# A bound for the first head from key maxima and weight-column lengths, with the opening of an attention kernel re-ordered around it

## The chip, the cores and the metric

The kernel runs on one core of a Trainium2 chip. A core has TensorE (PE, with its weight loads listed as PEld), VectorE (DVE), ScalarE (ACT), GpSimd (POOL) and SyncE (SP), which run side by side and wait for each other through semaphores, and 16 DMA engines. The metric is the device time of one execution in microseconds; the lower the better. Times of the timeline below are microseconds from the first instruction of the profiled execution.

## The reference

```python
xn = layernorm(x)                                   # x: 2048 x 640, eps 1e-5, no gain or offset
q = (xn @ wq).reshape(B, Sq, 32, 192).transpose(0, 2, 1, 3)
scores = einsum("bhqd,bhkd->bhqk", q, k_cache) * 192 ** -0.5
p = softmax(scores)
o = einsum("bhqk,bhkd->bhqd", p, v_cache)           # 32 heads, 2048 cached keys and values of 192
s = o.transpose(0, 2, 1, 3).reshape(B, Sq, 32 * 192) @ wo
h = silu(x @ w1) * (x @ w3)                         # called with xn in the place of x; 1536 wide
g = silu(h @ w2)
out = x + s * g
```

All tensors are bfloat16. x and the caches are normal numbers times 0.05; `wq` is normal times 0.05 over the root of 640.

## The kernel before, in words

**Softmax with a bound.** The kernel doesn't look for the maximum of each row of scores. It computes one number per head that no score exceeds in size, subtracts it inside the exponential, and divides by the sum of the exponentials at the end (the ones column of `vt` collects that sum). The bound is the sum over the 192 dimensions of (largest |k| of the dimension) x (largest |q| of the dimension), times the scale 192 ** -0.5 and a slack of 1.03. A second, exact path at the end of the program (`redo`) runs only where a sum of exponentials has become too small.

**Tiling.** Keys of a head are held transposed in `KT`, 128 partitions x 3 x 1024. Since 192 isn't a multiple of 128, two keys share a column: block 0 holds dimensions 0 to 127 of the even keys, block 1 dimensions 128 to 191 of the even keys and 0 to 63 of the odd ones, block 2 dimensions 64 to 191 of the odd ones. `KM` holds the two half blocks that have to lie on the other 64 partitions; POOL copies them (`copy_low` L139, `copy_high` L142). Queries are made per chunk of 512 rows of x: `project_chunk` (L348) multiplies the weights with `xnT`, the normalised and transposed x, and leaves `qA` (dimensions 0 to 127), `qF` (dimensions 128 to 191, beside 64 columns of the feed-forward weights), and copies on other partitions `qS` and `qD`. A step of attention is a pair of key tiles: `scores` (L508) is three pairs of 64-row matmuls into a PSUM tile `st2` of 1024 columns, `weights` (L530) is one exponential of it on ACT, and `values` (L561) are 32 matmuls of 193 columns that use the exponentials as weights. One block is eight such steps (512 queries against 2048 keys); a head has four blocks, and there are 32 heads. `advance` (L587) keeps the values two or three halves behind the scores.

**PSUM.** `st2` tiles come from a ring of two and serve the scores, the projections (`ps`) and the transposes of x (`pst`). The tags `ob0` and `ob1` hold the value sums; before the first values they serve other things: `ob1` is `fill`, the target of matmuls that only keep PE going, then `ahead`, then `third`; `ob0` is `bp`, half of the first projection.

**What sets the order.** Nearly every instruction of the first head is pinned (`pin`), so each engine issues in the order in which the program lists it. Each engine has one queue, SP and POOL issue DMAs from theirs, and an instruction that waits holds everything behind it.

**The opening.** x is loaded by tiles of 128 rows. DVE takes mean and variance (`ln_stats`), ACT makes the reciprocal root by a Ln and an Exp (`ln_root`), DVE scales (`ln_scale`), and PE and ACT transpose (`ln_turn`). Tiles 0 to 3 make chunk 0. `lead` (L648) runs the first five steps of head 0 and between them prepares tiles 4 to 7; tiles 8 to 15 are transposed by DMA from SP (`ln_send` L289) for later chunks. Chunk 0 of head 0 is projected at L363, 20 matmuls of 256 columns; then five matmuls `ahead` (L619) make `qA` of head 1's chunk 0. The first bound takes the key maxima (L404, DVE), the query maxima of chunk 0 straight from PSUM (L393), a shift between partition halves on POOL (`turned_shift` L425), their product (`first_product`), and a matmul with ones that sums over partitions and leaves the sum on all of them (`first_bound` L459). Chunks 1 to 3 get bounds of their own from `next_bound` (L479), with an all-reduce over partitions on POOL (L476). `posts` and `extra_at` (L679, L689) list what is put behind which step: chunk 1 is projected at step (0, 5), head 1's first chunk at (1, 1).

Of the kernel before, what the change touches and what calls it, by code (L numbers as in the profile page):

```python
# [30 lines left out]
def _kernel_impl(ctx, tc, A_x, A_k_cache, A_v_cache, A_wq, A_wo, B_w1, B_w3, B_w2, out):  # L31
# [57 lines left out]
    def load_weights(h):  # L89
# [5 lines left out]
        if h == 0:  # L95
# [7 lines left out]
            return dict(wq=(columns(1), columns(0)), next_wA=columns(2),  # L103
                        pieces=[lambda: piece(A_wq[:, 0:DH + P], PGW, PGW + DH + P), lambda: piece(wsel[:, 0:PGW], 0, PGW)])
# [54 lines left out]
    with ExitStack() as actx:  # L159
# [44 lines left out]
        def load_cols(out, w):  # L204
            pin(nc.gpsimd.dma_start(out=out, in_=w.rearrange("(c p) d -> p c d", p=P)))

        loads[0] = load_keys(0, [first_w["pieces"][0], lambda: [f() for f in first_w["pieces"][1:]], lambda: [load_x(nc.sync, *t) for t in ((4, 6), (6, 8), (8, 12))]])
        loads[0].update(first_w)
        load_x(nc.sync, 12, 16)
# [107 lines left out]
        def start_head(h):  # L317
# [9 lines left out]
            pin((nc.gpsimd if h == 1 else nc.vector).memset(heads[h]["st"][:], 0.0))  # L327
# [20 lines left out]
        def project_chunk(h, qb, cast=nc.vector.tensor_copy, mid=()):  # L348
# [8 lines left out]
            elif h == 0:  # L357
                acc["bp"] = ps_o.tile([P, 2, 512], F32, tag="ob0", name="bp")
# [20 lines left out]
            else:  # L379
                pin(cast(out=qA[:, qs], in_=halves[0]))  # L380
                pin(cast(out=qF[:, qs], in_=halves[1]))
            keep = pin if h == 0 or h == 1 else (lambda x: x)
            first = h == 0 and qb == 0
            copy = nc.scalar.copy if first else nc.gpsimd.tensor_copy
            for t in range(2):
                keep((copy if t == 0 else nc.gpsimd.tensor_copy)(out=qS[ROWS[t], qs], in_=qA[ROWS[1 - t], qs]))  # L386

            keep(copy(out=qD[:, qs], in_=qF[PGW:P, qs]))

            def maxima():  # L390
                cA, cF = (4, 3) if h == 0 else (3, 4)
                for col, src, r0 in ((cA, halves[0] if first else qA[:, qs], 0), (cF, halves[1] if first else qF[:, qs], PGW)):
                    pin(nc.vector.tensor_reduce(out=st[r0:P, col, qb:qb + 1], in_=src[r0:P, :], axis=AX.X, op=ALU.max,  # L393
                                                apply_absolute_value=True))
# [30 lines left out]
        def turned_shift():  # L425
            m = heads[0]["st"][:, 0:3, 0]
            sh = stt.tile([P, 2], F32, tag="sh", name="sh")
            pin(nc.gpsimd.memset(sh[ROWS[0], 0:1], 0.0))

            def down():  # L430
                pin(nc.gpsimd.tensor_copy(out=sh[ROWS[1], 1:2], in_=m[ROWS[0], 1:2]))

            def rest():
                pin(nc.gpsimd.tensor_copy(out=sh[ROWS[0], 1:2], in_=m[ROWS[1], 0:1]))
                pin(nc.gpsimd.tensor_copy(out=sh[ROWS[1], 0:1], in_=m[ROWS[0], 0:1]))  # L435

            def join():
                km = stt.tile([P, 2], F32, tag="km", name="km")
                pin(nc.vector.tensor_tensor(out=km[:], in0=m[:, 1:3], in1=sh[:], op=ALU.max))
                return km  # L440
            return down, rest, join

# [9 lines left out]
        def first_product():  # L452
            hd = heads[0]
            pr = stt.tile([P, 2], BF16, tag="prb", name="prb")
            pin(nc.vector.scalar_tensor_tensor(out=pr[:], in0=hd["km"][:], scalar=-SCALE * SLACK,
                                               in1=hd["st"][:, 3:5, 0], op0=ALU.mult, op1=ALU.mult))
            return pr

        def first_bound(pr):  # L459
            hd = heads[0]  # L460
            bp = acc["bp"]
            for t in range(2):
                pin(nc.tensor.matmul(bp[:, 0, 0:1], lhsT=ones_bf[:], rhs=pr[:, t:t + 1], start=(t == 0), stop=(t == 1)))
            nb = stt.tile([P, 1], F32, tag="nbb", name="nbb")
            pin(nc.vector.tensor_copy(out=nb[:], in_=bp[:, 0, 0:1]))
            hd["nb"] = [nb]
# [11 lines left out]

        def next_bound(qb):  # L479
# [717 lines left out]
```

## Time and profile before

| | us |
|---|---|
| median of 3 runs | 1936.65 |
| lowest and highest of them | 1936.47, 1936.83 |
| the profiled execution | 1935.99 |
| span of the profiled execution, first to last instruction | 1934.4 |
| PE busy | 1927.3 |
| ACT busy | 1214.5 |
| DVE busy | 1090.5 |
| POOL busy | 460.1 |

The granted clock of TensorE was 1.00 throughout. A row of the timeline gives start, duration, engine, source line, operation, output and inputs with partitions x elements, how many were merged into it (x), and in brackets the idle time of the engine just before it and what ended that. Matmuls are pipelined: a matmul's shown duration includes the time in which its results drain while the next one already streams, so the distance of starts tells what one costs. A few matmul records are missing from the trace. The chain that ended last is found by going back from the last instruction, at each step to what released it or to the instruction before it on its engine. Groups by line give count, busy time in all, mean duration in ns, and the idle time before them.

### The profile page before, as it was taken

Reading aid. Unit: us, or ns where it says so; the run is one execution under the profiler, and the core shown is the slowest. Engines: PE = TensorE matmul, PEld = TensorE weight load, DVE = VectorE, ACT = ScalarE, POOL = GpSimd, SP = SyncE. Lnnn points to the kernel's source line nnn. Section 1 sums busy time; section 2 is a strip of 40 time slices with the busy share of each in tenths; the row PEclk is TensorE's granted clock in tenths of the full one; section 3 lists DMA queues with packets and bytes.
Section 4 is the critical chain, followed back from the end, with each engine's and each line's share of the span. In section 5 each row is a group of like instructions: output and inputs, shape, how many; then the busy total and the mean of one; then the engine's idle time right before and its main releaser. Section 6 shows DMA issues by size and latency. Waiting matters only on the chain.

```text
span 1934.4 us, 59509 instructions
## 1 busy us (share of the span) xinstructions
PE 1927.3 (100%) x26711; PEld 1264.6 (65%) x26734; DVE 1090.5 (56%) x2239; ACT 1214.5 (63%) x1177; POOL 460.1 (24%) x759
## 2 busy tenths in 40 slices
PE   9999999999999999999999999999999999999999
PEld 5666666666666666666667766666666666454446
DVE  8665656565656565666655666656665655521111
ACT  7777777777767677777777777777777777210000
POOL 3532222222222222233222222222222220000000
PEclk9999999999999999999999999999999999999999
DMA  7721223121212222232222222212131102937763
GB/s 172 140 71 42 80 42 79 42 73 37 59 40 66 51 56 62 58 95 68 63 50 71 50 71 48 73 42 79 41 79 35 46 10 84 268 92 143 167 147 82
DMA packets 339810, 148.62 MB, mean 77 GB/s; under 512 B 290384, under 2 KB 333008, under 8 KB 339552
## 3 DMA queue, kind: packets, MB, share of 16 engines
q1 hardware_dynamic: 326496, 115.00, 25.7%
q0 software_dynamic: 8352, 24.75, 4.8%
q10 hardware_dynamic: 4704, 5.05, 0.8%
q8 instruction: 209, 3.42, 0.8%
q14 instruction: 49, 0.40, 0.1%
HBM read 54.59 MB, written 31.98 MB: 45 GB/s over the span
## 4 chain that ended last, share of the span: by engine, by line
PE 99%; SPq 0%; DMA 0%; ACT 0%; issue 0%; DVE 0%; POOL 0%
PE obank L572 35%; PE st L526 34%; PE ps L374 14%; PE ps_s L941 8%; PE ps_s L897 3%; PE ps_f L961 2%; PE ps_gu L754 1%; PE ps_f L977 1%; PE ps L779 0%; PE ps L338 0%; DMA KT<-in_A_k_cache_dram 0%; SPq L119 0%; PE ps_gu L338 0%; ACT xnT L281 0%; PE pst L280 0%
## 5 line engine op out<-in xcount | busy, mean ns | idle before, releaser
L532 ACT ACTIVATE pT<-st,nb 128x1024 bf16<-128x1024 f32 x1016 | 1130.6, 1113 | 435.4 <-PE st L526 435.0
L572 PEld LDWEIGHTS <-pT 64*128 64x128 bf16 x16384 | 713.3, 94 | 243.0 <-ACT pT L532 1.9
L572 PE MATMUL obank<-vt,pT 64*128 64x193 bf16 x16384 | 852.4, 243 | 0.2 <-ACT pT L532 0.2
L542 DVE COPY osum<-obank 128x386 f32<-128x386 f32 x256 | 142.2, 556 | 551.3 <-PE obank L572 551.3
L526 PE MATMUL st<-qS,KM 64*128 64x512 bf16 x1023 | 384.7, 376 | 0.1
L526 PE MATMUL st<-qA,KM 64*128 64x512 bf16 x1023 | 384.7, 376 | 0.0
L526 PE MATMUL st<-qA,KT 64*128 64x512 bf16 x1023 | 384.7, 376 | 0.0
L526 PE MATMUL st<-qS,KT 64*128 64x512 bf16 x1023 | 384.7, 376 | 0.0
L526 PE MATMUL st<-qF,KT 64*128 64x512 bf16 x1023 | 384.7, 376 | 0.0
L526 PE MATMUL st<-qD,KT 64*128 64x512 bf16 x1023 | 384.6, 376 | 0.0
L386 POOL COPY qS<-qA 64x512 bf16<-64x512 bf16 x255 | 188.8, 741 | 503.8 <-DVE qA L380 478.1
L526 PEld LDWEIGHTS <-KT 64*128 64x128 bf16 x4096 | 201.6, 94 | 136.1 <-issue 0.6
L374 PE MATMUL ps<-xnT,wq 64*128 64x512 bf16 x1230 | 285.7, 376 | 0.0
L374 PE MATMUL ps<-xnS,wq 64*128 64x512 bf16 x1230 | 284.6, 376 | 0.0
L374 PEld LDWEIGHTS <-wq 64*128 64x128 bf16 x2460 | 119.2, 94 | 115.6
L549 DVE TENSOR_TENSOR ostage<-osum,rl_all 128x384 bf16<-128x384 f32 x256 | 152.6, 596 | 8.8
L941 PE MATMUL ps_s<-oT,wo_sb 128*128 128x512 bf16 x705 | 154.9, 379 | 0.8
L543 DVE TENSOR_TENSOR osum<-osum,obank 128x386 f32<-128x386 f32 x256 | 142.6, 557 | 8.9
L941 PEld LDWEIGHTS <-wo_sb 128*128 128x128 bf16 x720 | 70.4, 98 | 84.9 <-issue 0.2
L404 DVE TENSOR_REDUCE st<-KT 128x1 f32<-128x512 bf16 (+1 forms) x189 | 122.1, 685 | 1.4 <-DMA KT<-in_A_k_cache_dram 0.2
L526 PEld LDWEIGHTS <-KM 64*128 64x128 bf16 x2048 | 100.6, 94 | 16.2 <-POOL sh L435 0.4
L108 POOL DMA_DIRECT2D wq<-in_A_wq_dram x62 | 45.5, 734 | 272.5 <-PE ps L374 250.6
(148 smaller groups left out, 1180.9 us busy)
## 6 DMA issues: line engine op xcount, KB each, us to landing
o_scr<-ostage SPq DMA_DIRECT2D x64, 384.0 KB, 2.7
vt<-in_A_v_cache_dram SPq DMA_DIRECT2D x62, 384.0 KB, 4.9
wo_sb<-in_A_wo_dram POOLq DMA_DIRECT2D x1, 7680.0 KB, 31.7
wq<-in_A_wq_dram POOLq DMA_DIRECT2D x31, 160.0 KB, 3.2
hT_scr<-hblk SPq DMA_DIRECT2D x16, 256.0 KB, 3.1
xnS<-xnT POOLq DMA_DIRECT2D x8, 320.0 KB, 5.7
wq<-in_B_w_dram POOLq DMA_DIRECT2D x31, 80.0 KB, 2.6
wq<-in_A_wq_dram POOLq DMA_DIRECT2D x31, 80.0 KB, 2.9
```

The costliest lines, as they stand in the source:

```text
L108: keep(nc.gpsimd.dma_start(out=wq[ROWS[t], :, c0:c1], in_=w.rearrange("(s p) d -> p s d", p=DT)))
L374: pin(nc.tensor.matmul(halves[t], lhsT=wq[ROWS[t], s, :], rhs=xs[ROWS[t], s // 2, qs], start=(s == 0), stop=(s == 2 * DC - 1)))
L386: keep((copy if t == 0 else nc.gpsimd.tensor_copy)(out=qS[ROWS[t], qs], in_=qA[ROWS[1 - t], qs]))
L404: pin(nc.vector.tensor_reduce(out=heads[h]["st"][:, j, k:k + 1], in_=heads[h]["L"]["KT"][:, j, c0:c1], axis=AX.X, op=ALU.max, apply_absolu ...
L526: pin(nc.tensor.matmul(st2[:, t * 512:(t + 1) * 512], lhsT=k, rhs=q[ROWS[t], qs], start=(s == 0), stop=(s == 2)))
L532: pin(nc.scalar.activation(out=pT2[:], in_=st2[:], func=ACT.Exp, scale=SCALE, bias=nb[:]))
L542: pin(nc.vector.tensor_copy(out=osum[:], in_=ov[:, 0, :, 0:DH + 1]))
L543: pin(nc.vector.tensor_tensor(out=osum[:], in0=osum[:], in1=ov[:, 1, :, 0:DH + 1], op=ALU.add))
L549: pin(nc.vector.tensor_tensor(out=ostage[:, b * 2:b * 2 + 2, hg * DH:(hg + 1) * DH], in0=osum[:, :, 0:DH], in1=rl.unsqueeze(2).to_broadcas ...
L572: pin(nc.tensor.matmul(acc["o"][b][:, r, (j % 2) * 256:(j % 2) * 256 + DH + 1], lhsT=pT2[ROWS[r], t * 512 + j * P:t * 512 + (j + 1) * P], ...
L897: pin(nc.tensor.matmul(ps, lhsT=oT[:, k, :], rhs=wo_sb[:, k, c0:c1], start=(k == 0), stop=(k == OC - 1)))
L941: pin(nc.tensor.matmul(ps_of[d], lhsT=wo_sb[:, k, d * P:(d + 1) * P], rhs=part(k // KQ)[:, k % KQ, :], start=(k == 0), stop=(k == OC - 1)))
```

## The change

The bound of head 0 no longer looks at queries. A row of the normalised x has a squared length of at most 640, so no |q| of a dimension exceeds the root of 640 times the length of that dimension's column of `wq`. The lengths come from squares of the weights (ACT for 128 columns, POOL for 64), 20 one-column matmuls against ones that sum the squares over the 640 rows, and a Ln and an Exp with factor one half for the root. One bound then holds for all four chunks of head 0, so the query maxima of head 0, the shift between partition halves and `next_bound` go. Even and odd keys get sums of their own, in two banks of `fill`, and the smaller of the two (the larger bound, since they are negative) is taken.

Around that:

- `ahead` goes into the second half of the projection's own tile `ps`, which is unused since the other half of the projection is in `bp`; before, it had a tile of its own in `ob1`.
- For chunk 0 the two `qS` copies run on DVE (before: one on ACT, one on POOL) and the `qD` copy on POOL (before: ACT).
- For chunk 1 of head 0 the cast of `qF` runs on DVE (before: ACT).
- The scaling and transposes of tiles 8 and 9 (`ln_send` 8) and the second half of tile 11's statistics move from inside and behind the projection of chunk 1 to behind step (0, 5).
- `next_wF` and the weights of head 1 are loaded from SP's queue (before: POOL's), `next_wF` ahead of the last x tiles and the weights behind them; x tiles 8 to 15 come in five pieces instead of two.
- The warm-up all-reduce on POOL now takes `wn`, and it and the first `swap_rows` stand before the first scores (before: after the third step).
- The memset of head 0's `st` goes.

```diff
-                keep(nc.gpsimd.dma_start(out=wq[ROWS[t], :, c0:c1], in_=w.rearrange("(s p) d -> p s d", p=DT)))
+                keep((nc.sync if h == 1 else nc.gpsimd).dma_start(out=wq[ROWS[t], :, c0:c1], in_=w.rearrange("(s p) d -> p s d", p=DT)))
...
-        loads[0] = load_keys(0, [..., lambda: [load_x(nc.sync, *t) for t in ((4, 6), (6, 8), (8, 12))]])
+        loads[0] = load_keys(0, [..., lambda: [load_x(nc.sync, *t) for t in ((4, 6), (6, 8), (8, 10), (10, 12))]])
         loads[0].update(first_w)
-        load_x(nc.sync, 12, 16)
+        load_cols(next_wF[:, :, 0:PGW], B_w3[:, 0:PGW])
+        load_cols(next_wF[:, :, PGW:P], A_wq[:, DH + P:2 * DH])
+        for t0, t1 in ((12, 14), (14, 15), (15, 16)):
+            load_x(nc.sync, t0, t1)
+        loads[1] = load_weights(1)
...
-                pin(cast(out=qF[:, qs], in_=halves[1]))
+                pin((nc.vector.tensor_copy if h == 0 and qb == 1 else cast)(out=qF[:, qs], in_=halves[1]))
...
-                keep((copy if t == 0 else nc.gpsimd.tensor_copy)(out=qS[ROWS[t], qs], in_=qA[ROWS[1 - t], qs]))
-            keep(copy(out=qD[:, qs], in_=qF[PGW:P, qs]))
+                keep((nc.vector if first else nc.gpsimd).tensor_copy(out=qS[ROWS[t], qs], in_=qA[ROWS[1 - t], qs]))
+            keep(nc.gpsimd.tensor_copy(out=qD[:, qs], in_=qF[PGW:P, qs]))
...
+        def weight_squares():
+            wq = first_w["wq_all"][:, :, PGW:PGW + DH]
+            sq = lnx.tile([P, DC, DH], BF16, name="sq")
+            pin(nc.scalar.activation(out=sq[:, :, DT:DH], in_=wq[:, :, DT:DH], func=ACT.Square))
+            pin(nc.gpsimd.tensor_tensor(out=sq[:, :, 0:DT], in0=wq[:, :, 0:DT], in1=wq[:, :, 0:DT], op=ALU.mult))
+            return sq
+
+        def weight_norms(sq):
+            ns = fill[:, 1, 0:3]
+            for rows_, j, k0 in ((slice(0, P), 2, DT), (slice(0, P), 0, 0), (ROWS[0], 1, P), (ROWS[1], 1, 0)):
+                for c in range(DC):
+                    pin(nc.tensor.matmul(ns[rows_, j:j + 1], lhsT=sq[:, c, k0:k0 + rows_.stop - rows_.start], rhs=ones_bf[:, 0:1],
+                                         start=(c == 0), stop=(c == DC - 1)))
+            lw = stt.tile([P, 3], F32, tag="lw", name="lw")
+            pin(nc.scalar.activation(out=lw[:], in_=ns, func=ACT.Ln, bias=eps_t[:], scale=1.0))
+            wn = stt.tile([P, 3], F32, tag="wn", name="wn")
+            pin(nc.scalar.activation(out=wn[:], in_=lw[:], func=ACT.Exp, scale=0.5))
+            return wn
+
+        def first_product(wn):
+            pr = stt.tile([P, 3], BF16, tag="prb", name="prb")
+            pin(nc.vector.scalar_tensor_tensor(out=pr[:], in0=heads[0]["st"][:, 0:3, 0], scalar=-SCALE * SLACK * float(D) ** 0.5,
+                                               in1=wn[:], op0=ALU.mult, op1=ALU.mult))
+            return pr
...
+            sums = [fill[:, t, 8:9] for t in range(2)]
             for t in range(2):
-                pin(nc.tensor.matmul(bp[:, 0, 0:1], lhsT=ones_bf[:], rhs=pr[:, t:t + 1], start=(t == 0), stop=(t == 1)))
+                pin(nc.tensor.matmul(sums[t], lhsT=ones_bf[:], rhs=pr[:, 2 * t:2 * t + 1], start=True, stop=False))
+            for t in range(2):
+                pin(nc.tensor.matmul(sums[t], lhsT=ones_bf[ROWS[t], :], rhs=pr[ROWS[t], 1:2], start=False, stop=True))
             nb = stt.tile([P, 1], F32, tag="nbb", name="nbb")
-            pin(nc.vector.tensor_copy(out=nb[:], in_=bp[:, 0, 0:1]))
-            hd["nb"] = [nb]
+            pin(nc.vector.tensor_reduce(out=nb[:], in_=fill[:, :, 8], axis=AX.X, op=ALU.min))
+            heads[0]["nb"] = [nb] * NQB
...
+        sq = weight_squares()
         copy_low(L0)
         key_maxima(0, 0)
-        rest_of_shift()
-        project_chunk(0, 0, nc.scalar.copy)()
-        heads[0]["km"] = join()
+        project_chunk(0, 0, nc.scalar.copy)
         set_ones(L0)
...
         start_head(1)
-        pr = first_product()
-        ahead = ps_o.tile([P, 2, 512], F32, tag="ob1", name="ahead")
+        wn = weight_norms(sq)
+        warm = stt.tile([P, 1], F32, tag="warm", name="warm")
+        pin(nc.gpsimd.partition_all_reduce(warm[:], wn[:, 0:1], P, bass_isa.ReduceOp.add))
+        swap_rows(0)
+        pr = first_product(wn)
+        ahead = acc["ps"][:, 512:1024]
...
-        early = [scores(heads[0], 0, 0)]
-        first_bound(pr)
+        early = [scores(heads[0], 0, 0, hook=lambda: first_bound(pr))]
...
         posts = {
-            (0, 5): ((ln_send, 10, 1),),
+            (0, 5): ((ln_send, 8), (ln_send, 10, 1), (ln_half, 11, 1)),
...
-            (0, 5): ((first_project, 0, 1, (ln_root, 8, 3), (ln_send, 8)),),
+            (0, 5): ((first_project, 0, 1, (ln_root, 8, 3)),),
```

The hook of the first `scores` runs `first_bound` between its first and its second pair of matmuls.

More of the change, by code (lines that the diff above doesn't have):

```diff
@@ L423, in join_maxima @@
             return km
[L425 to L441, printed above, removed]
         def key_shift(h):
@@ L506, in swiglu_chunk, with scores @@
             return product
-        def scores(hd, qb, p, fill=(0, 0, 0), st2=None):
+        def scores(hd, qb, p, st2=None, hook=None):
             KT, KM = hd["L"]["KT"], hd["L"]["KM"]
@@ L523, in scores @@
             for s, step in enumerate(steps):
-                keep_busy(fill[s])
+                if hook and s == 1:
+                    hook()
                 for t, (k, q) in enumerate(step):
@@ L636, in first_project @@
             maxima = project_chunk(h, qb, nc.scalar.copy, mid)
-            if h == 0:
-                maxima()
-                if qb == 1:
-                    ln_half(11, 1)
-                next_bound(qb)
-            else:
+            if h:
                 behind.append(maxima)
@@ L656, in lead @@
             ln_root(4, 4)
-            warm = stt.tile([P, 1], F32, tag="warm", name="warm")
-            pin(nc.gpsimd.partition_all_reduce(warm[:], rstd[4], P, bass_isa.ReduceOp.add))
-            heads[1]["L"].update(load_weights(1))
-            swap_rows(0)
             st2 = scores(hd, 0, 4)
```

33 lines of the change are left out of this document (9 added, 24 removed).

## The prediction

> **What bounds the kernel now.** I read the busy line and the chain that ended last first, then the chain in order of time, and then the rows of the first 45 us, because only there does the order of instructions change: behind head 0 every engine's list is the same as before.
>
> ```profile
> span 1934.4 us, 59509 instructions
> PE 1927.3 (100%) x26711; PEld 1264.6 (65%) x26734; DVE 1090.5 (56%) x2239; ACT 1214.5 (63%) x1177; POOL 460.1 (24%) x759
> ...
> PE 99%; SPq 0%; DMA 0%; ACT 0%; issue 0%; DVE 0%; POOL 0%
> ```
>
> TensorE (PE) is busy for 1927.3 of 1934.4 us and carries 99% of the chain. One row of the chain in order of time, repeated, shows the steady pace:
>
> ```profile
> 74.86 2.16 PE ps L374 x20
> 87.53 2.16 PE ps L374 x20
> ```
>
> A block of eight key pairs takes 87.53 - 74.86 = 12.67 us, all of it on PE. Work taken off VectorE (DVE), ScalarE (ACT) or GpSimd (POOL) gains there only where PE waits for it, and a TensorE instruction added is paid in full unless it stands in such a wait. So the sum is made of two stretches in which PE does wait: from the first projection to the first exponentials, and from 26 to 31 us. The first, by start and duration in the timeline:
>
> ```profile
> 11.91 0.58 ACT L380 CAST qA<-ps 128x512 bf16<-128x512 f32 x1 [1.01 <-PE ps L363]
> 12.26 1.24 PE L619 MATMUL ahead<-xnT,wq 128*128 128x512 bf16 x4
> 13.29 0.61 POOL L386 COPY qS<-qA 64x512 bf16<-64x512 bf16 x1
> 13.43 0.39 PE L526 MATMUL st<-qA,KM 64*128 64x512 bf16 x1
> 13.52 0.70 DVE L393 TENSOR_REDUCE st<-bp 64x1 f32<-64x512 f32 x1
> 13.96 0.37 PE L526 MATMUL st<-qS,KM 64*128 64x512 bf16 x1
> 14.11 0.57 ACT L620 CAST qA<-ahead 128x512 bf16<-128x512 f32 x1
> 14.69 0.20 PE L463 MATMUL bp<-prb,ones_bf 128*128 128x1 bf16 x2
> 14.93 0.16 DVE L465 COPY nbb<-bp 128x1 f32<-128x1 f32 x1 [0.33 <-PE bp L463]
> 15.13 2.12 ACT L532 ACTIVATE pT<-st,nbb 128x1024 bf16<-128x1024 f32 x2 [0.44 <-DVE nbb L465]
> 16.30 0.51 PE L572 MATMUL obank<-vt,pT 64*128 64x193 bf16 x8
> ```
>
> PE has finished `ahead` at about 13.3 and issues the first score pair in halves, at 13.43 and 13.96, because its second half needs `qS`, whose POOL copy ends at 13.90. The bound is late too: query maxima on DVE until 14.22, product, PE at 14.69, copy until 15.09, and only then the first exponential (15.13). PE gets its first weights at 16.30. A 512-column matmul is shown with 0.37 to 0.39 but gives way sooner: `ahead` is five matmuls (one record is missing) from 12.26 to 13.50, so four steps to the last start and one duration of 0.38 make a step (1.24 - 0.38) / 4 = 0.215 us.
>
> **The change, stretch one.** Added on PE: 20 matmuls of one column each (norms of the weight columns) between the projection and `ahead`, and four instead of two for the bound. Added on ACT: one square over 640 elements a partition, a Ln, an Exp. Added on POOL: a product over 320 elements. Their nearest rows:
>
> ```profile
> 5.30 0.29 ACT L253 ACTIVATE lv<-mv,eps_t 128x1 f32<-128x1 f32 x1 [0.31 <-DVE mv L225]
> 5.63 0.20 ACT L260 ACTIVATE rstd<-lv 128x1 f32<-128x1 f32 x1
> 5.74 0.81 ACT L243 ACTIVATE junk<-x_all,nmean 128x640 bf16<-128x640 bf16 x1
> 11.70 1.04 POOL L139 COPY KM<-KT 64x1024 bf16<-64x1024 bf16 x1 [1.14 <-DMA KT<-in_A_k_cache_dram]
> 18.30 2.18 PE L572 MATMUL obank<-vt,pT 64*128 64x193 bf16 x48
> 20.41 1.32 PE L280 MATMUL pst<-ident_bf,xn 128*128 128x128 bf16 x20
> ```
>
> The square costs about 0.81 (the square of 128x640). ACT is idle for 1.01 before its cast at 11.91, so it lies in that gap at no cost; if it ran over by 0.2, the cast would be late by that and nothing would wait, since DVE reads `qA` only after its key maxima at about 12.9. The POOL product has no row. POOL has been idle for 1.14 before the second key copy at 11.70; a copy of 1024 elements takes 1.04, so 320 elements with two inputs are bounded by about 0.3 and 1.0, both hidden; a longer one would push that key copy, which ends at 12.74, some 1.5 before PE reads it.
>
> The 20 one-column matmuls have no row as a group. Each loads its own weights. From below, the 48 of 193 columns take 2.18, or 0.045 each, two side by side. From above, the pair at 14.69 gives way to the next scores at 14.83 (the row of 14.69 says 0.20 for both with their tail), and 20 transposes take 1.32 or 0.066 each. That is 0.9 to 1.3 us; I take 0.9, as one column streams less than the 193 that make up the lower row. A smaller cost isn't excluded, so the low end of the range uses 0.5, the nearest row halved. The Trainium skill, TensorE: Matmul & The Clock Gate, section "Back-to-back issue gap", gives about 81 ns for a stream of weight load and matmul at 128 columns, and its section "Wait — 56ns, not 53.3ns?" a floor of about 25 ns between starts; as estimates these would be 1.6 and 0.5 us here. The transposes at 0.066 speak against the first of them.
>
> With N for that time the order after it is: `ahead` 12.26+N to 13.34+N (five steps of 0.215), the first score pair until 13.55+N, four bound matmuls at 0.045 until 13.73+N, two pairs until 14.16+N, readable 0.17 later. The Ln (0.29) and Exp (0.20) run beside `ahead`; the product of 0.16 follows at about 13.2+N, ahead of its use at 13.55+N; the minimum over both banks ends near 14.1+N. The first exponential therefore starts at 14.37+N, set by the scores and no longer by the bound: 15.27 with N = 0.9, against 15.13. What was a wait for `qS` and for the bound is now filled with norms. The two `qS` copies move to DVE behind its key maxima, 12.9 to about 13.6, in time for 13.34+N; `qD` moves to POOL after `qF` at 13.05, there by 13.7 to 14.1 and needed at 13.94+N. `ahead` in the free half of `ps` makes the second score tile wait until ACT has copied it (13.5+N plus 0.57): 14.1+N, when PE arrives at 14.16+N. Stretch one: **+0.14**, ends -0.3 (N = 0.5) and +0.5 (N = 1.3). The layer norm chain behind it follows ACT's exponentials and shifts by the same.
>
> **Stretch two.** The rows from 26 to 31, and the cast on DVE from the groups by line:
>
> ```profile
> 25.94 0.58 ACT L380 CAST qA<-ps 128x512 bf16<-128x512 f32 x1 [0.29 <-PE ps L338]
> 26.43 0.59 ACT L381 CAST qF<-ps 128x512 bf16<-128x512 f32 x1
> 26.66 1.25 POOL L386 COPY qS<-qA 64x512 bf16<-64x512 bf16 x2
> 26.90 2.14 ACT L532 ACTIVATE pT<-st,nbb 128x1024 bf16<-128x1024 f32 x2
> 27.07 0.37 PE L526 MATMUL st<-qA,KM 64*128 64x512 bf16 x1
> 27.97 0.61 POOL L388 COPY qD<-qF 64x512 bf16<-64x512 bf16 x1
> 28.00 0.49 DVE L223 BATCH_NORM_STATS2 st<-x_all 128x6 f32<-128x320 bf16 x1
> 28.09 0.51 PE L572 MATMUL obank<-vt,pT 64*128 64x193 bf16 x8 [0.19 <-ACT pT L532]
> 28.53 0.21 DVE L225 BATCH_NORM_AGGREGATE mv<-st 128x2 f32<-128x12 f32 x1
> 29.49 0.45 DVE L271 TENSOR_SCALAR xn<-x_all,mv,rstd 128x640 bf16<-128x640 bf16 x1 [0.19 <-ACT rstd L260]
> 29.58 2.13 ACT L532 ACTIVATE pT<-st,nb 128x1024 bf16<-128x1024 f32 x2
> 29.61 1.45 POOL L386 COPY qS<-qA 64x512 bf16<-64x512 bf16 x2
> 30.75 1.26 PE L368 MATMUL ps<-xnT,next_wF 64*128 64x512 bf16 x10
> ```
>
> ```profile
> L381 DVE CAST qF<-ps 128x512 bf16<-128x512 f32 x120 | 81.6, 680 | 0.0
> ```
>
> Half the cast of chunk 1 (0.59 on ACT) goes to DVE, where it takes 0.68. It starts after ACT's `qA` cast at 26.53 (in the changed order its one wait is for ACT) and ends at 27.23, not 27.02. ACT's exponential starts at 26.55, not 26.90, so the wait of PE at 28.09 goes: 27.66 is early enough. But three things come next. The score tile that reuses the projection's bank, issued at 27.07, must now wait for DVE: 27.28. It ends at 27.93, so PE gains only 28.09 - 27.93 = 0.16. Second, on DVE the normalisations of tiles 8 to 10 (0.45 each, 0.36 apart) no longer run before the cast but behind it, until 28.4, then the half statistics (0.49) and the aggregate (0.21), so `mv` is ready at 29.1 and not at 28.74. Third, ACT holds its exponentials behind the Ln of that `mv`: Ln at 29.15, exponential at 29.6, where it now starts at 29.58. The projection at 30.75 waits for the bank that this exponential frees. So the gain of 0.16 is lost again at 30.75: **0.0** if nothing else happens. The removed all-reduces of the query bound only took 0.1 of ACT's wait there.
>
> What else can happen is that DVE and POOL hold each other up. POOL's copies of `qS` take 1.25 for two at 26.66 but 1.45 at 29.61, where the first begins 0.12 after a normalisation has begun on DVE (29.49): 0.20 longer. In the new order three normalisations stand exactly over `qS` and `qD` (27.3 to 28.6). The Trainium skill, SBUF — State Buffer, section on who interferes with whom, says that such a VectorE instruction and any GpSimd one exclude each other for the whole instruction; 0.20 here agrees with it. Bounds from the rows: none, 0.0; one hold of 0.20 for each of two pairs moves `mv` by 0.4 and so the projection to 31.15; if the two engines alternate in full, DVE loses two copies of about 0.5 and the projection comes 1.1 late. I take the middle, **+0.4**.
>
> **Parts without a price.** Eight query reductions (0.70 each) leave DVE and three all-reduces POOL; PE waited for none of them after 30 us. The warm-up all-reduce and the two swaps go ahead of the weights' loads, from 22.6 and 25.2 to about 14; POOL is idle there and the next POOL work that PE needs is `qS` at 26.66. SP issues the 128 columns of `next_wF` and the three pieces of head 1 weights instead of POOL, and x in smaller pieces: five more issues of 0.5 ahead of the transposes of tiles 8 on, whose first was issued at 26, so they fall in SP's idle time. The value rows of pairs 4 to 7 are issued 0.5 later and now share the engines with the swaps:
>
> ```profile
> 11.54 1.06 SPq L122 DMA_DIRECT2D vt<-in_A_v_cache_dram  x2
> 21.67 0.51 PE L572 MATMUL obank<-vt,pT 64*128 64x193 bf16 x8
> ```
>
> ```profile
> DMA to landing us min/median/max: 3.9/5.0/6.2
> ```
>
> They landed at most 6.2 after issue, that is by 18.3, and are read from 21.67: 3.4 us of cover. Without that cover each further us would be one on PE. The transposes of tiles 8 to 11 start 1.5 later, but no longer beside the weight loads; used at 35.8.
>
> **Sum.** +0.14 + 0.4 = +0.5. The profiled execution took 1935.99 (span 1934.4 and 1.6 around it), 0.66 under the median of 1936.65; it would be 1936.5, and the median **1937.2 us**. About 0.2% (3.9 us) is what counts here as a difference, so this is no change.
>
> **Rivals.** (a) No net effect, 1936.65 within 0.3: the norms take 0.75 and DVE and POOL don't meet. For: PE's share of 100%; against: the row at 29.61. (b) Faster, 1935.9: N = 0.5 (-0.3), no holds, and the transfer of the cast keeps 0.4 since the exponential isn't behind the Ln; for: the wait of 0.4 before 28.09; against: the order on ACT. It can't reach 0.2%, as PE's waits in the two stretches (about 0.5 around 13.43 to 13.96, 0.2 at 14.69, 0.2 at 16.30, 0.4 at 28.09) sum to about 1.3, and 0.5 must be paid. (c) Slower: the swaps and weights put ahead hold back the value rows. It decides where these take over 9.6 us to land (12.05 to 21.67): at twice the longest, 12.4, PE stands still for 2.8 us, 1939.9, and at 13.8 it would be over 0.2%. Against: 6.2 was the most. (d) Full alternation in stretch two with N = 1.3: +1.6, 1938.2.
>
> **Chances.** Forecast (+0.2 to +1.2) 0.48; (a) 0.22; (b) 0.15; (d) 0.10; (c) 0.05, of which 0.03 beyond 0.2%. For 8 in 10 the range takes in (a), (d) and most of (b): 1935.8 to 1938.3. Faster by over 0.2% 0.015, the same 0.95, slower 0.035.
>
> **What the changed profile would show.** Right: the norms end about 0.9 after 12.26, no split first score pair, the first exponential at 15.2 to 15.4; a POOL copy near 27.3 longer than 0.8, the Ln of tile 11 after 29.1, and the projection of `next_wF` at about 31.3. Wrong: norms under 0.6 or over 1.4; POOL copies of 0.61 throughout with the projection before 30.7; PE idle before 21.67 on value rows; any difference behind 45 us, where the block should still take 12.67.

## The result and the profile after

The changed kernel takes 1948.49 us (median; 1945.11 to 1951.60), the kernel before 1936.56 beside it: a ratio of 1.0061, interval 1.0048 to 1.0074. It is slower by 12 us, where no change was forecast. The page of the changed kernel, its busy line, its chain by engine and one group by line:

```profile
span 1946.9 us, 59553 instructions
PE 1931.4 (99%) x26756; PEld 1332.2 (68%) x26756; DVE 1085.6 (56%) x2226; ACT 1214.9 (62%) x1177; POOL 452.8 (23%) x748
PE 98%; DMA 1%; DVE 0%; ACT 0%; POOL 0%; issue 0%; POOLq 0%
L380 PE MATMUL ps<-xnS,wq 64*128 64x512 bf16 x1230 | 283.1, 378 | 9.2 <-DMA xnS<-xnT 9.2
```

The span has grown by 12.5 us, the busy time of PE by 4. The share of DMA in the chain has risen from 0% to 1%, and the group says which transfer it is: the projections of later heads, which read `xnS` (the normalised x with its halves of partitions swapped), waited 9.2 us for the DMA that writes it. In the kernel before the same group has no wait:

```profile
L374 PE MATMUL ps<-xnS,wq 64*128 64x512 bf16 x1230 | 284.6, 376 | 0.0
```

The timeline of PE puts the wait in one place, head 1's projection of chunk 3 at step (3, 4); first the kernel before, then the changed one:

```profile
65.96 0.38 PE L374 MATMUL ps<-xnT,wq 64*128 64x512 bf16 x1
65.97 0.59 PE L374 MATMUL ps<-xnS,wq 64*128 64x512 bf16 x2
...
67.91 0.38 PE L374 MATMUL ps<-xnT,wq 64*128 64x512 bf16 x1
```

```profile
66.23 0.38 PE L380 MATMUL ps<-xnT,wq 64*128 64x512 bf16 x1
75.76 0.61 PE L380 MATMUL ps<-xnS,wq 64*128 64x512 bf16 x2 [9.15 <-DMA xnS<-xnT]
76.13 0.66 PE L380 MATMUL ps<-xnT,wq 64*128 64x512 bf16 x2
76.56 0.66 PE L380 MATMUL ps<-xnS,wq 64*128 64x512 bf16 x2
...
79.54 0.38 PE L380 MATMUL ps<-xnT,wq 64*128 64x512 bf16 x1
```

Until there the change has cost 0.27 us (66.23 against 65.96). The first matmul on `xnS` comes 9.79 later than before, so the wait is worth 9.5. Then the nine pairs up to the last row take 3.78 us instead of 1.94, a pair each 0.42 instead of 0.215: another 1.84. At 79.54 the kernel is 11.63 behind, and that is nearly all of the 12.5. The windows of the changed kernel (busy time of PE, PEld, DVE, ACT, POOL, then the granted clock, the DMA engines' busy share and GB/s) show both terms:

```profile
55.00:60.00 5.00, 5.00 (x86) 3.52 (x82) 1.59 (x4) 4.42 (x5) 4.84 (x7) 1.00 1.25 208
60.00:65.00 5.00, 5.00 (x74) 3.10 (x70) 4.82 (x10) 3.36 (x5) 4.08 (x8) 1.00 1.28 113
65.00:70.00 5.00, 1.60 (x25) 0.89 (x22) 1.47 (x4) 2.08 (x2) 0.08 (x1) 0.93 1.30 105
70.00:75.00 5.00, 0.00 (x0) 0.00 (x0) 0.00 (x0) 0.00 (x0) 0.00 (x0) 0.50 0.62 119
75.00:80.00 5.00, 4.24 (x24) 1.77 (x25) 0.00 (x0) 0.04 (x1) 0.00 (x0) 0.55 0.06 14
```

PE, DVE, ACT and POOL stand still from 70 to 75, the clock falls to 0.50 in the wait and stays low for 3.8 us after PE has resumed. The DMA engines are busy all through 55 to 70, but from 60 on they move only 113 and 105 GB/s, where the kernel before moves 140 and 190 in the same windows. The Trainium skill, TensorE: Matmul & The Clock Gate, section "Wait — 56ns, not 53.3ns?", gives 426.7 ns for a 512-column matmul at the cold clock and 215.7 at the warm one; the pairs here (0.42 and 0.215) agree.

What kept the DMA? The timelines of 50 to 60 us, before and after, with the rows that issue it (`xnS<-xnT`, the swap of chunk 3) and the key transposes of head 2 (`KT`, from SP):

```profile
54.31 0.69 DVE L393 TENSOR_REDUCE st<-qA 128x1 f32<-128x512 bf16 x1 [1.97 <-ACT qA L380]
55.03 0.68 DVE L393 TENSOR_REDUCE st<-qF 64x1 f32<-64x512 bf16 x1
55.75 0.54 DVE L470 SCALAR_TENSOR_TENSOR pr<-km,st 128x2 f32<-128x2 f32 x1
...
57.33 1.37 POOL L400 DMA_DIRECT2D xnS<-xnT  x2 [0.22 <-issue]
...
58.48 0.06 DVE L717 MEMSET KT<- 128x3 uint32 x1
58.57 16.55 SPq L119 DMA_TRANSPOSE KT<-in_A_k_cache_dram  x2
```

```profile
54.61 0.06 DVE L706 MEMSET KT<- 128x3 uint32 x1
54.70 7.28 SPq L119 DMA_TRANSPOSE KT<-in_A_k_cache_dram  x1
56.55 1.33 POOL L403 DMA_DIRECT2D xnS<-xnT  x2
```

The transposes of head 2 wait for a small memset on DVE. Before, DVE first did the query maxima of head 0's chunk 3, for which it waited until 54.31, and the product and reduction of its bound; the memset came at 58.48, behind the swap (57.33). The change took that work off DVE, the memset ran 3.9 us sooner, and the transposes went ahead of the swap, whose own issue hardly moved. The chain of the changed kernel gives the price, 18.50 us from issue to landing where the swaps before took 6.1 to 8.0:

```profile
57.21 18.50 DMA xnS<-xnT
75.71 0.04 issue
75.76 4.17 PE ps L380 x19
```

So **theory T**: less work on VectorE released head 2's key transposes ahead of the swap; its packets waited with theirs, and PE paid 9.5 us of standing still and 1.8 of half clock. **Rivals**: R1, the loads and swaps that the change moved delay this swap; R2, the norms, the bound and the cast cost it in many small places.

### The profile page after: what moved, and what is told of

It is laid out like the page before. It is cut to its first block, busy times and chain, and to the rows that moved or that the text cites. A ratio compares the mean times of both kernels' runs of the same rounds, so it can differ in the third digit from the quotient of the medians.

```text
span 1946.9 us, 59553 instructions
## 1 busy us (share of the span) xinstructions
PE 1931.4 (99%) x26756; PEld 1332.2 (68%) x26756; DVE 1085.6 (56%) x2226; ACT 1214.9 (62%) x1177; POOL 452.8 (23%) x748
## 4 chain that ended last, share of the span: by engine, by line
PE 98%; DMA 1%; DVE 0%; ACT 0%; POOL 0%; issue 0%; POOLq 0%
PE obank L573 34%; PE st L527 34%; PE ps L380 14%; PE ps_s L930 8%; PE ps_s L886 3%; PE ps_f L950 2%; PE ps_gu L743 1%; DMA xnS<-xnT 1%; PE ps_f L966 1%; PE ps L768 0%; PE ps L343 0%; PE fill L219 0%; PE pst L284 0%; PE ps_gu L343 0%; DVE xn L275 0%; ACT xnT L285 0%
## 5 line engine op out<-in xcount | busy, mean ns | idle before, releaser
L533 ACT ACTIVATE pT<-st,nb 128x1024 bf16<-128x1024 f32 x992 | 1104.7, 1114 | 431.4 <-PE st L527 430.8
L573 PEld LDWEIGHTS <-pT 64*128 64x128 bf16 x16384 | 746.6, 94 | 209.6 <-ACT pT L533 0.9
L573 PE MATMUL obank<-vt,pT 64*128 64x193 bf16 x16384 | 870.7, 243 | 0.0
L527 PEld LDWEIGHTS <-KT 64*128 64x128 bf16 x4096 | 232.0, 94 | 119.0 <-issue 0.2
L380 PEld LDWEIGHTS <-wq 64*128 64x128 bf16 x2460 | 136.5, 94 | 111.8 <-issue 11.5
L527 PEld LDWEIGHTS <-KM 64*128 64x128 bf16 x2048 | 116.1, 94 | 14.8 <-issue 0.5
```

The lines of the kernel that those rows point to most:

```text
L380: pin(nc.tensor.matmul(halves[t], lhsT=wq[ROWS[t], s, :], rhs=xs[ROWS[t], s // 2, qs], start=(s == 0), stop=(s == 2 * DC - 1)))
L527: pin(nc.tensor.matmul(st2[:, t * 512:(t + 1) * 512], lhsT=k, rhs=q[ROWS[t], qs], start=(s == 0), stop=(s == 2)))
L533: pin(nc.scalar.activation(out=pT2[:], in_=st2[:], func=ACT.Exp, scale=SCALE, bias=nb[:]))
L573: pin(nc.tensor.matmul(acc["o"][b][:, r, (j % 2) * 256:(j % 2) * 256 + DH + 1], lhsT=pT2[ROWS[r], t * 512 + j * P:t * 512 + (j + 1) * P], ...
```

## The experiments

**Keys late in the changed kernel.** The memset and the key transposes of head 2 move from behind pair 6 of chunk 2 to behind pair 0 of chunk 3, behind the weights of head 2.

```diff
                 if (qb, p) in ((1, 5), (1, 6), (1, 7)):
                     heads[1]["L"]["rest"].pop(0)()
-                if (qb, p) == (2, 6):
-                    loads[2] = load_keys(2, hold=True)
+                if (qb, p) == (2, 7):
+                    copy_keys(heads[1]["L"])
+                    loads[2] = load_weights(2)
+                if (qb, p) == (3, 0):
+                    loads[2].update(load_keys(2, hold=True))
                     pin(nc.vector.memset(loads[2]["KT"][:, :, 0:2], 0.0))
                     loads[2]["rest"].pop(0)()
-                if (qb, p) == (2, 7):
-                    copy_keys(heads[1]["L"])
-                    loads[2].update(load_weights(2))
```

> The changed kernel, with one thing moved: the memset of the two first columns of the key tile of head 2 and the key transposes that wait for it stand behind pair 0 of query chunk 3 instead of pair 6 of chunk 2, so behind the swap of rows of chunk 3. Theory T (the freed VectorE starts these transposes 3.9 us sooner, ahead of the swap, whose packets then take 18.5 us): the swap lands 6 to 9 us after its issue as before, the projection of head 1 chunk 3 starts at 66.1 to 66.6, TensorE's clock stays at 1.0 there, and the time is 1936.7 to 1937.3. Rival R1 (the loads of head 1, now on SyncE's queue, or the earlier swaps slow this swap): the stall of 9.3 us at 66 stays, 1948. Rival R2 (the norms, the bound or the cast cost it in many small places): no stall but still above 1945.

Measured: 1937.21 us, ratio to before 1.0005 (0.9996 to 1.0015). Its timeline:

```profile
56.39 1.33 POOL L403 DMA_DIRECT2D xnS<-xnT  x2
60.67 0.39 PE L380 MATMUL ps<-xnS,wq 64*128 64x512 bf16 x2 [0.33 <-DMA xnS<-xnT]
61.09 0.06 DVE L709 MEMSET KT<- 128x3 uint32 x1
61.18 5.41 SPq L119 DMA_TRANSPOSE KT<-in_A_k_cache_dram  x1
```

The swap at 56.39 lands in time and nothing waits at 66; the one wait left, 0.33, is for an earlier swap. With everything else of the change in place the 11 us are gone: R1 and R2 alone can't be their cause.

**Keys early in the kernel before.** The same memset and transposes, in the kernel before, ahead of `advance` of step (2, 4).

```diff
+                if (qb, p) == (2, 4):
+                    loads[2] = load_keys(2, hold=True)
+                    pin(nc.vector.memset(loads[2]["KT"][:, :, 0:2], 0.0))
+                    loads[2]["rest"].pop(0)()
                 ex = extra_at.get((qb, p))
                 advance(heads[0], qb, p, steps(*ex) if ex else None)
...
-                if (qb, p) == (2, 6):
-                    loads[2] = load_keys(2, hold=True)
-                    pin(nc.vector.memset(loads[2]["KT"][:, :, 0:2], 0.0))
-                    loads[2]["rest"].pop(0)()
```

> The kernel before, with one thing moved: the memset and key transposes of head 2 stand ahead of pair 4 of chunk 2 instead of behind pair 6, so that they are issued about 5 us sooner, at 52 to 54, ahead of the swap of chunk 3 (57.3). Nothing else of the change is in it. Theory T: the swap lands at 71 to 76 instead of 65.9, the projection that starts at 66.13 waits 5 to 10 us for it and then runs about 2 us longer at half clock: 1943 to 1949. Rivals R1 and R2: neither the loads nor the norms are touched, so 1936.5, within 0.5.

Measured: 1943.38 us, ratio 1.0029 (1.0019 to 1.0039); single runs from 1936.6 to 1944.8. In the profiled one (span 1940.2) the chain reads:

```profile
57.32 12.74 DMA xnS<-xnT
70.10 3.92 PE ps L374 x19
```

The stall and the half clock (3.92 instead of 2.16) appear without anything else of the change. The size is smaller and varies from run to run: here PE waited 4.5 us, although the transposes were issued 4.1 us ahead of the swap (52.50 against 56.62) and only 1.9 ahead in the changed kernel. So the early transposes alone are enough for a stall, but why the wait is twice as long in the changed kernel isn't shown; the loads that the change moved (R1) may have a part in that.

**VectorE's work put back.** The most direct test of T's first link: only the two query reductions of chunk 3 come back, and nobody reads them.

```diff
             if h:
                 behind.append(maxima)
+            elif qb == 3:
+                maxima()
```

> The changed kernel, with only the two query reductions of head 0 chunk 3 back on VectorE (their results aren't used). No load, no swap and no wait is moved in the program. Theory T: VectorE waits for the casts of that projection again (until 54.3), does 1.4 us more, and reaches the memset of the keys of head 2 at 57.2 to 58.0 instead of 54.61; the transposes are issued behind the swap (56.6 and 57.2), the swap lands by 67, the stall at 66 is gone or under 1.5 us, and work added makes the kernel faster: 1936.7 to 1938.5. If VectorE's saved time isn't the cause, 1948 to 1950.

Measured: 1938.20 us, ratio 1.0011 (1.0001 to 1.0020): 1.4 us of useless work make the kernel 10 us faster. Its runs go from 1937.21 (the profiled one) to 1941.27. Its timeline has the order of the kernel before again:

```profile
54.70 0.69 DVE L396 TENSOR_REDUCE st<-qA 128x1 f32<-128x512 bf16 x1 [1.97 <-ACT qA L386]
55.40 0.68 DVE L396 TENSOR_REDUCE st<-qF 64x1 f32<-64x512 bf16 x1
56.60 1.32 POOL L403 DMA_DIRECT2D xnS<-xnT  x2
58.12 0.06 DVE L708 MEMSET KT<- 128x3 uint32 x1
58.21 8.30 SPq L119 DMA_TRANSPOSE KT<-in_A_k_cache_dram  x1
```

**The swap first.** The other way to restore the order: the transposes stay early, the swap is moved ahead of them.

```diff
-            (2, 4): ((swap_rows, 3),),
+            (2, 3): ((swap_rows, 3),),
```

> The changed kernel, with the swap of rows of chunk 3 posted behind pair 3 of chunk 2 instead of pair 4, ahead of the three copies of the projection on GpSimd; the key transposes stay early, at 54.7. Theory T: the swap is issued at 51 to 53, ahead of the transposes, lands by 62, no stall, 1936.7 to 1937.3; if the order of issue doesn't matter and any transposes in flight delay it, it lands after 70 and the time stays above 1943. R1: it takes 18 us wherever it stands, lands at 70, 1942. R2: 1948.

Measured: 1940.29 us, ratio 1.0019 (1.0009 to 1.0029). The swap was issued at 51.0 and is no longer waited for, but the time is 3 us above what T had said. The chain shows the next in line, the weights of head 2, which POOL issues at 58.6 to 60.1:

```profile
60.08 16.15 DMA wq<-in_A_wq_dram
76.36 2.32 PE ps L380 x19
```

They are needed at 74.9 in the kernel before and land at 76.2. PE waited 1.0 us for them and another 1.5 at 86.9, for which the profile names no cause. So T was too narrow: whatever is issued behind these transposes is late, and the keys themselves took 24.1 us here. What helps is to issue the transposes later, not one victim sooner.

**Transposes or any load?** First, the value rows of head 2 were to take the place of the transposes.

```diff
                 if (qb, p) == (2, 6):
                     loads[2] = load_keys(2, hold=True)
-                    pin(nc.vector.memset(loads[2]["KT"][:, :, 0:2], 0.0))
-                    loads[2]["rest"].pop(0)()
+                    loads[2]["rest"].pop()()
+                    loads[2]["rest"].pop()()
                 if (qb, p) == (2, 7):
                     copy_keys(heads[1]["L"])
                     loads[2].update(load_weights(2))
+                if (qb, p) == (3, 0):
+                    pin(nc.vector.memset(loads[2]["KT"][:, :, 0:2], 0.0))
+                    loads[2]["rest"].pop(0)()
```

> The changed kernel, with the value rows of head 2 (two plain loads of 384 KB) issued at the place where its key transposes stood, and the memset and transposes behind pair 0 of chunk 3. What goes ahead of the swap is thus 768 KB of plain rows instead of the transposes. If the transposes are what holds the swap (their packets are under 512 bytes and the engines move 105 to 113 GB/s with them, against 240 without): the swap lands within 9 us of its issue, no stall, 1936.7 to 1937.5. If any load ahead of it does: the swap lands after 68, PE waits 2 us or more, 1939 to 1945.

Measured: 1937.36 us, ratio 1.0004 (0.9994 to 1.0014). It answers less than it was meant to: SP's list starts these value rows between 47 and 53 us in every kernel here, also where the program names them later, so the edit left the list of the late keys unchanged and only repeats that run. The next one does ask the question, with one plain load of the same 768 KB behind the same memset:

```diff
+            if h == 2:
+                rows = A_k_cache[0, h].rearrange("(p s) d -> p (s d)", p=P).rearrange("p (j n) -> p j n", j=3)
+                rest[0] = lambda: keep(nc.sync.dma_start(out=KT[:], in_=rows))
```

> The changed kernel, with the key transposes of head 2 replaced, at the same place and behind the same memset, by one plain load of the same 768 KB (6 KB in a row for each partition). Head 2 then computes with keys that aren't transposed, so the output isn't the reference's; every instruction on the other engines stays. If it's the transposes that hold the swap (in the changed kernel the engines move 105 to 113 GB/s beside them, against 240 just before): the swap lands within 10 us of its issue at 56.6, no stall at 66, 1936.7 to 1937.7. If any 768 KB issued ahead of the swap holds it: the swap lands after 68, PE waits 2 us or more, 1939 to 1948.

Measured: 1938.83 us, ratio 1.0011 (1.0002 to 1.0020), between the two expectations. Two windows, the two waits of PE and the landing times of the swaps:

```profile
60.00:65.00 5.00, 4.25 (x57) 2.66 (x53) 4.35 (x10) 2.57 (x4) 3.09 (x6) 1.00 1.08 300
65.00:70.00 5.00, 4.31 (x56) 2.81 (x53) 1.89 (x4) 2.76 (x3) 0.98 (x2) 1.00 0.45 93
61.10 0.39 PE L383 MATMUL ps<-xnS,wq 64*128 64x512 bf16 x2 [0.75 <-DMA xnS<-xnT]
68.06 0.39 PE L383 MATMUL ps<-xnS,wq 64*128 64x512 bf16 x2 [0.69 <-DMA xnS<-xnT]
DMA to landing us min/median/max: 6.8/10.6/11.0
```

The plain load is issued at 54.55, as early as the transposes, and the swap behind it takes 11.0 us at most and costs PE 0.69 us of waiting, at 68.06. The wait at 61.10 is for the swap of chunk 2, which was issued 4 us ahead of the load. So the order of issue counts for a plain load too, but little: the engines move 300 GB/s from 60 to 65. With the transposes in its place they move 113 and 105, and the swap takes 18.5 (17.4 in the next experiment). The times agree: the highest run here, 1940.07, is below the lowest of the changed kernel, 1945.11. How much later the transposes make a swap isn't fixed, though: in the kernel before with early keys it was 12.7.

**The stall filled.** 44 matmuls ahead of the waiting projection, into the bank that it overwrites.

```diff
+                if h == 1 and qb == 3:
+                    for i in range(44):
+                        pin(nc.tensor.matmul(halves[0], lhsT=wq[:, 0, :], rhs=xnT[:, 0, qs], start=True, stop=True))
```

> The changed kernel, with 44 more matmuls of 512 columns (0.215 us each, 9.5 us) ahead of the projection of head 1 chunk 3, into the half bank that the projection overwrites; they need only rows that are there. Theory T with the clock as its second term (stall 9.3 us, and 2.0 us since the projection and what follows it run at half clock until 79.5): the dummies fill the stall, the projection still starts at 75.7 but takes 2.16 and not 4.17, the clock stays at 1.0, and the time falls by 1.5 to 2.3, to 1946.2 to 1947.0. If the lower clock is not a consequence of the stall, 4.17 stays and so does the time, 1948.5; if the packets weren't what the projection waits for, the dummies come on top, 1958.

Measured: 1947.01 us, ratio 1.0059 (1.0042 to 1.0075), 1.5 below the changed kernel's 1948.49. In the window 75 to 80 the clock is 1.00:

```profile
75.00:80.00 5.00, 5.00 (x59) 2.67 (x59) 1.05 (x2) 1.70 (x3) 0.99 (x2) 1.00 0.18 22
```

PE busy with dummies for 9.60 us costs the kernel no more than PE standing still: the half clock is a consequence of the stall, and worth 1.5 to 1.8 us. The intervals of the two kernels overlap, so the trace (the projection in 2.27 instead of 4.17) decides here, not the time.

**Stretch two: the cast back on ScalarE**, in the kernel of the late keys.

```diff
-                pin((nc.vector.tensor_copy if h == 0 and qb == 1 else cast)(out=qF[:, qs], in_=halves[1]))
+                pin(cast(out=qF[:, qs], in_=halves[1]))
```

> The kernel of the late keys (the changed kernel with the keys of head 2 behind pair 0 of chunk 3), with half of the cast of head 0 chunk 1 back on ScalarE as before the change. By the prediction's stretch two (VectorE's normalisations behind the cast and over GpSimd's copies cost 0.4 to 0.5): the normalisations run at 0.45 each again, and the projection with the next head's weights starts at 30.5 to 30.7 instead of 31.1. If it's the order of the other steps there (transposes issued later, loads on SyncE's queue), it stays at 31.0 to 31.2. The time differs by half a microsecond from 1937.2 at most, less than the measurement can tell; the start of that projection decides.

Measured: 1936.90 us, ratio 1.0003 (0.9993 to 1.0013). From the start of chunk 1's projection to that of the next head's, this kernel takes 30.35 - 22.73 = 7.62; the changed kernel takes 31.07 - 23.00 = 8.07, and so do all six others with its cast on VectorE. The three normalisations take 1.16 here and 1.75 there.

**The cast alone on VectorE, in the kernel before.**

```diff
-                pin(cast(out=qF[:, qs], in_=halves[1]))
+                pin((nc.vector.tensor_copy if h == 0 and qb == 1 else cast)(out=qF[:, qs], in_=halves[1]))
```

> The kernel before, with only half of the cast of head 0 chunk 1 on VectorE. By the prediction's stretch two: the three normalisations stand over GpSimd's copies and take 1.5 to 1.8 instead of 1.2, the statistics behind them are ready later, and the projection with the next head's weights starts at 31.1 to 31.3 instead of 30.75; 1936.4 to 1937.4. If the cast costs nothing or gains, that projection starts at 30.3 to 30.8.

Measured: 1938.05 us, ratio 1.0008 (0.9998 to 1.0017). The stretch takes 30.60 - 22.40 = 8.20 instead of the 7.64 before, but not as expected: in this order the normalisations stand ahead of the cast and don't meet POOL's copies. The cast's 0.69 pushes the query maxima and the statistics behind it. One caution: with late keys and no cast (the next kernel) the stretch took 8.14 in its profile, as GpSimd's all-reduce came late there, so this one reading doesn't settle the price in the old order. Another 1.0 of the 1.8 us is the collision again: PE waited 0.6 for the swap and 0.4 for the weights, although the transposes were issued at 58.62 as before.

**Keys late in the kernel before**, with the very edit of the first experiment.

> The kernel before, with only the memset and key transposes of head 2 behind pair 0 of chunk 3 instead of pair 6 of chunk 2 (from 58.5 to about 61). Theory T and the trace of the kernel before (its swap lands at 65.9 and is used at about 66, its weights of head 2 land at 70.9 and are used at 74.9): nothing waits there in the profiled run, so 1935.7 to 1936.5, at most 0.5 better where single runs lost a little to this collision, and the highest run below 1938. If the order of loads there costs the kernel before something in each run, 1934 to 1935.5. If later keys cost head 1 its key maxima, above 1937.

Measured: 1935.90 us, ratio 0.9995 (0.9986 to 1.0004); the highest run is 1936.35, where the kernel before beside it reached 1940.09. A gain can't be told from none. Its median is the lowest of these kernels, and it lacks the change.

## Why the prediction was wrong

- **The step that failed** is in "Parts without a price": "Eight query reductions (0.70 each) leave DVE and three all-reduces POOL; PE waited for none of them after 30 us." That is true and not enough. The prediction read the rows of the first 45 us, "because only there does the order of instructions change"; but head 0 runs on past 70 us, and in the kernel before the work that the change removes stands on VectorE's list until 56.55. The question was what stands behind them on VectorE's list: a memset of 0.06 us that lets SyncE start 768 KB of transposes. Work taken away was costed at nothing where it moved a transfer by 3.9 us; keys late, keys early and the reductions put back show it from three sides.
- **A cover that was not looked up.** In the kernel before the second of the two swap DMAs is issued at 58.03 and lands at 65.9, and the projection reads it at 65.97: no cover to speak of. Only the first swap's place was named in the prediction.
- **Rival (c)** had the kind right (loads moved ahead hold back a transfer that PE needs, at 12 us and more to land) and the place wrong: value rows at 21.67, with the price of 1939.9. From 9 to 66 us PE waited for no DMA in the changed kernel, so the loads on SyncE's queue did cost nothing. The value rows landed within 6.2 us, as before. The all-reduce and the two swaps that the prediction put at about 14 ran at 20.05 and 20.33: that reading of POOL's list was wrong, though nothing came of it. The chance of 0.05 was for that one place; no rival asked which DMAs are released by the engines that get work taken off.
- **Its own alarm**, "any difference behind 45 us, where the block should still take 12.67", is what rang.
- **Stretch one** (+0.14). The rows that answer to those of before:

```profile
12.04 0.70 PE L448 MATMUL fill<-ones_bf,sq 128*128 128x1 bf16 x20
12.67 1.25 PE L618 MATMUL ps<-xnT,wq 128*128 128x512 bf16 x5
14.53 0.16 DVE L469 TENSOR_REDUCE nbb<-fill 128x1 f32<-128x2 f32 x1 [1.02 <-PE fill L467]
14.98 2.12 ACT L533 ACTIVATE pT<-st,nbb 128x1024 bf16<-128x1024 f32 x2 [0.44 <-PE st L527]
```

  The norms take 12.67 - 12.04 = 0.63 and not 0.9, under the 0.9 to 1.3 of its two rows but inside the ends 0.5 and 1.3 of the range; the first exponential waits for the scores and not for the bound, as said, at 14.98 instead of 15.27. (The sum's 14.16 + 0.17 is 14.33 and not 14.37; the trace has 0.20 from the last pair to the exponential, 14.78 to 14.98, so the 14.37 does hold.) That is 0.15 sooner than in the profile before, where a gain of up to 0.3 was the low end. Against other profiles it is a loss: from the first projection to the first exponential the old opening took 5.32 in that profile and 4.95 to 4.99 in three others, the new one 5.1 to 5.2 in seven and 5.5 in one. That these differ by about the +0.14 of the forecast is luck: the norms were 0.27 shorter than the sum has them, and the profile on which the sum rests showed an old opening some 0.35 longer than the other three.
- **Stretch two** (+0.4, as a hold between VectorE and GpSimd):

```profile
26.55 1.41 POOL L391 COPY qS<-qA 64x512 bf16<-64x512 bf16 x2 [4.50 <-ACT qA L386]
27.06 1.75 DVE L275 TENSOR_SCALAR xn<-x_all,mv,rstd 128x640 bf16<-128x640 bf16 x3
29.49 0.29 ACT L257 ACTIVATE lv<-mv,eps_t 128x1 f32<-128x1 f32 x1 [0.32 <-DVE mv L229]
31.07 0.61 PE L374 MATMUL ps<-xnT,next_wF 64*128 64x512 bf16 x4 [0.35 <-ACT pT L533]
```

  Right in size (8.07 against 7.62, +0.45) and, in this order of instructions, in mechanism: normalisations over POOL's copies, the Ln waiting for `mv`, the exponential and the projection behind it. The hold between the two engines is read from these durations (1.75 against 1.16 for the normalisations); no run varied it by itself.
- **Sum.** With the collision taken out the change is worth 1937.21 against 1936.37 beside it. The forecast of +0.5 is near that kernel's 0.84, and the measurement can't tell either from no change (the ratio's interval is 0.9996 to 1.0015). That its 1937.2 is met to the digit is luck, as the last point shows.
- **What stays open.** In the profiles the changed kernel is 11.6 behind the kernel before at 137 us, 12.2 at 870 and 11.8 at the last exponential; the late keys are 0.7, 1.5 and 1.1 behind in the same places, while the kernel before with late keys keeps its 0.3 throughout. From the last exponential to VectorE's last instruction all twelve kernels take 287.9. From there to the end of the span the four with the old opening take 2.4 to 2.5 and the eight with the new one 2.9 to 3.3: 0.4 to 0.9 us are lost behind the last computation, where only the last rows are stored, for a reason that no run here looked for. No term of the prediction covers that. Nor is it settled why the same transposes take 12.6 us in the kernel before and 18.2 with the cast alone on VectorE, issued at the same place; in the latter the value rows ahead of them were issued until 56.0 instead of 52.7, which no run tested as a cause.

## What to carry to other kernels

Work taken off an engine moves everything behind it on that engine's list forward, also the small instructions that release a DMA: look up what those transfers are and what the queue order becomes, above all where PE reads a transfer with less than a microsecond of cover. Where transfers compete, compare their landing time with the first use in the trace of before, for each of them and not only for the ones that the change names. Start slow transposes behind the transfers that are needed sooner, and by a dependence rather than by how long an engine happens to be busy; the runs here moved them by their place in the program and tried no such dependence.

## What the runs showed of the hardware

- DMA transposes of 768 KB from HBM took, from issue to landing, 9.6 us behind the swap (late keys; 10.1 to 10.6 in the other three kernels with late keys), 12.6 in the kernel before, 21.7 in the changed kernel and 24.1 with the swap first; 786,432 bytes over these times are 82, 62, 36 and 33 GB/s. The Trainium skill, DMA: Bandwidth & Descriptors, section "Latency and other measured facts", gives 261 GB/s, or 350 to 400 for the contiguous case; the measurement decides, and here it is far lower, with the wait in the queue and other transfers beside it counted in; no run here shows the transposes alone. Its section "Issuing engines are not separate DMA queues" says that DMAs of all engines end on the same 16 DMA engines and interleave: GpSimd's swap behind SyncE's transposes agrees with it.
- Issuing the transposes 3.9 us sooner made them land 5.2 us later (54.70 + 21.7 = 76.4 against 58.57 + 12.6 = 71.2). Early isn't only a change of order: from 60 to 70 us the engines moved 113 and 105 GB/s instead of 140 and 190.
- The clock fell to 0.50 in a wait of 9.2 us and came back 3.8 us after PE had resumed; matmuls that computed nothing through the wait kept it at 1.00.
- Weight load and matmul of one column, 20 in a row, cost 0.03 us each (0.63 over 20 in seven of the eight profiles with the norms, 0.82 in one).
